# Zero gaps between the score tiles of a fused attention and long-convolution kernel, with a rebuilt start and a new instruction order

## The chip, the cores and the metric

The kernel runs on one core of one Trainium2 chip. The metric is the time of one execution in microseconds (us), as a median of several runs. A second number, the span, is the time from the first to the last instruction in one profiled execution.

The core has a matrix engine (PE; its weight loads are shown apart as PEld), a vector engine (DVE), a scalar engine with lookup tables (ACT), a general engine (POOL) and an engine that only issues transfers (SP). POOL, SP and ACT can start DMA transfers.

## The reference

Four batches of 768 positions, 8 heads of 64. First a local attention with 8 global keys, then a gated long convolution.

```python
scores = scale * q @ k.T - slopes[h] * dist      # dist: position difference, or 96 for a global key
keep   = (key < 8) | ((0 <= rel) & (rel < 96))   # rel = query - key
x      = softmax(where(keep, scores, -1e9)) @ v  # heads side by side: [4, 768, 512]
x1, x2, x3 = split(x @ w_proj)                   # 512 columns each
y      = x1 * irfft(rfft(x2) * rfft(filter)) * x3
out    = y @ w_out
```

## The kernel before, in words

**Attention.** The keys of a batch are cut into seven tiles of 112 (K0); the upper 112 rows of a 128-row tile hold them, the lower 16 rows hold the 8 global keys and zeros. Queries that such a tile can see are at most 208, so its scores form a strip of 208 columns (96 for the last tile), and a head's strips stand side by side in the tensor E, 208 apart. Tiles come in three groups (GRP): 0 and 1; 2 and 3; 4, 5 and 6. For each group and pair of heads there is a step "scores" (PE), one "exp" (ACT, L711) and, from batch 1 on, a "masked" product with exp(-slope x distance) (DVE, L718). In batch 0 the masks don't exist yet, so the biases are added inside PE: L688 multiplies a scaled identity ("slope", L516 to L523) by copies of the distance table dg ("near", L505 to L514).

"values" (L728 to L743) multiplies strips by v, with the E strip as weights: for query tile t first 128 columns of strip t (L736), then, for t > 0, the last 96 columns of strip t-1 (L741), which land on rows 0 to 95 of the same bank.

**q and k** must be transposed to QT and KT. In batches 0 to 2 PE does it (L628 for the first tiles, which come as fp32; L661 for the rest). In batch 3 SP does it with transposing DMAs ("crossed", L650). QT and KT exist once, so a transposed tile may be written only when the batch before has read the old one. Parts of x are transposed by SP as well (L792).

**Convolution.** After attention come the gates (L827), the projection (L901), a transform as matrix products (L615), the products with the filter's spectrum on DVE, the inverse (L926, L929), and the output projection (L953); ACT and DVE empty the PSUM banks between them (L305, L309, L311, L836).

**Order.** Every step is an operation with a number, given by its place in the code. ORDER lists all of them by hand; "84P45" is operation 84 on engine P with PSUM banks 4 and 5, and the letters are P, A (ACT), V (DVE), G (POOL) and S (SP); "i22b0" is 22 idle matmuls. So ORDER fixes, for each engine, which steps it does and in which sequence, and an engine never passes a waiting step. Counting the operations through the code gives each number its name.

**Start.** DVE clears idle, the slope tensor, the lower rows of k and v (L392, L394, L1092) and the spare columns of E (L399); POOL builds an identity and dg (L479 to L486) and then issues loads; SP loads q tiles 2 and 1, k tile 0, the first rows of v and q tile 0; PE runs 22 idle matmuls. The first ACT step is a sine, which brings the sine table; the exp table follows at the first exp, the sine table again for the transform's tables (L420), and the exp table again for the masks (L539).

Of the kernel before, what the change touches and what calls it, by code (L numbers as in the profile page):

```python
# [11 lines left out]
BF16 = mybir.dt.bfloat16  # L12
# [4 lines left out]
P = 128  # L17
# [23 lines left out]
0V 1V 5G 2A 23G 32V 37A 41G 6A 7V 45G 46G 8V 40A 36A 9V 24V 33A 35A 47G 44G 11V 39A 25G 52G 50G 19S 51G 53G 13V 18S  # L41
26A 43G 29A 42G 49G 48G 58G 27A 17S i22b0 78P0 34A 74P1 10V 76P2 75V 77V 28V 56G 79A 55G 54G 3G 31V 57G 20S 254G 4V
80P0 30A 81A 16S 72P3 73A 82A 12V 38A 255G 104P1 105A i1b2 106P2 84P45 107V 108P3 109V 90P01 14V 83V 102P3 103V 59G
88P67 86P23 85A 89A 110P45 87A 15V 152P6 153V 148P7 149V 112P23 91A 111A 150P6 113A 114P01 115A 154P7 116P45 253G 21V
151V 155V 162P67 117A 63V 158P01 22V 97P45 98V 163A 99V 156P23 123P67 124V 159A 157A 68A 92P01 93V 125V 251G 94V 66A
118P45 119V 100P2 61G 101V 208P3 126P6 209A 120V 127A 213P7 160P01 95P2 214A 210V 121P6 96V 164P45 252G 122V 134P6
161A 169P01 128P2 211V 165V 166V 167P3 64A 212A 129P4 353P5 170V 215V 216V 217A 171V 136A 168V 172P0 133P3 71A 135A
220P1 221A 62G 70A 138P6 130A 354V 173V 179P3 175P0 131V 60G 201V 355A 180P5 69A 194V 202V 195V 197V 65A 203V 132V
262G 174P2 140A 204V 196V 198V 182A 222V 177A 263G 143P4 278P6 205V 219V 261G 223A 224A 349P0 145A 260G 266G 206V 137V
351P5 199V 287P7 207V 200V 276P4 225A 268G 181A 350V 352V 176A 279A 357P23 289P6 356A 218V 183V 277V 288A 274P7 363P45  # L50
226V 360P01 358A 67A 290A 484G 267G 364A 227V 359V 366P23 367A 291P6 292A 282P4 283A 228V 275A 256G 139P5 229V 381P6
382A 190P4 144P7 379P6 185P2 192A 230V 231V 232V 178V 425P4 233V 380V 234P3 269G 146A 257S 389P67 426V 141A 392P45
361A 259G 483G 187A 482G 386P01 362V 365V 265G 241P2 142V 242V 235A 184P3 393A 368V 264G 387A 388V 280P4 390A 281A
147V 236P2 427P5 186A 428V 429P0 430V 391V 189P1 374P45 375V 237A 481G 191A 383P67 440P23 480G 384A 293P0 258S 441A
489G 394V 376V 385V 581P1 294A 369P67 370V 239P4 582V 442V 240A 295P5 296A 371V 431P23 432A 395P01 396V 377P4 378A
490G 583V 492G 579P5 397V 577P6 580V 302P7 243V 303A 437P23 438A 434P01 578V 400P45 238V 372P7 401V 373A 402V 491G
607P6 435A 248P23 398P7 608V 403P4 404A 193V 609P5 272G 399V 300P6 249A 250A 271G 301A 270G 495G 439V 244P01 436V 245A
488G 406P4 420P2 421P3 707G 297V 708G 246A 610A 408A 433V 298V 423A 651P0 285V 448P67 449V 496G 652V 450V 410P1 588P45
411P3 188V 247V 304V 422A 412A 584A 589A 413A 443P01 444V 611P67 612A 445V 299V 585P45 415P2 586A 451P3 452A 416P6
591P45 592A 594P01 595A 305V 498G 446P7 447V 405P3 407A 473V 474V 417A 500G 320P4 321A 469P7 485G 705G 418A 312P5  # L60
620P01 313A 617P23 459P4 284V 471A 461A 419V 308P5 464P6 621A 618A 466A 497G 653P4 487S 316P7 317A 286V 310P0 475V
710G 476V 477V 306P1 716G 717G 309A 314P2 318P6 307A 319A 587V 706G 478V 519P7 493G 593V 463P1 479V 315A 409V 654A
655P6 656A 720G 590V 311V 465A 454P5 517P4 714G 805S 424V 614P01 520A 486S 804S 803S 666P23 725G 456A 660P67 502P5
414V 518A 661A 712S 830S 596V 322V 615A 468P4 323V 613V 667A 521P6 504P7 470A 505A 324V 657P01 616V 325V 709G 503A
806S 273G 668V 663P23 664A 523P4 515P7 831S 658A 828S 715G 453P5 455A 619V 326V 721G 506P2 507A 622V 718G 329V 330V
597P01 598V 522A 524A 327V 458P5 599V 460A 516A 494G 626P23 510P6 508P4 509A 802S 511A 627V 665V 328V 807V 829S 340P5
341A 628A 832A 600P4 601V 623P01 602P67 346P5 347A 603V 337P4 808P23 624V 338A 625V 604V 814P01 815A 662V 501G 811P67
659V 526V 874S 809A 530P5 525V 343P4 499G 669P01 722G 531A 812A 629S 816V 344A 672P23 331P5 332A 605P4 606A 457V 673V
670V 674V 528P6 529A 334P7 467V 833P45 817P23 671V 875S 335A 839P01 834A 818A 462V 810V 532V 630S 472V 873S 642P6 644A
646P7 648A 713G 527V 636P4 638A 813V 631P5 836P67 842P23 840A 512V 843A 533V 637P4 719G 639A 513V 647P0 649A 819V 711S  # L70
633A 723G 632P1 726G 641P4 837A 514V 844V 823P23 546P5 841V 643A 820P67 542P4 835V 824V 825V 675S 634A 848P01 547A
543A 548P5 333S 549A 544P4 876S 877A 540P2 821V 822V 849V 676S 850V 545A 650V 677S 698V 699V 701V 640V 645V 826S 827S
541A 534P3 535A 342S 887P67 881P45 884P01 888A 889V 694P2 689P3 536P6 882A 883V 700V 885A 679P7 681A 693P4 696A 838V
537A 695A 683P5 702V 724G 635V 538P7 539A 703V 684P2 688P4 690A 685A 886V 845P67 878P01 879A 731P4 846V 732A 550V 551A
678P5 847V 851S 880V 893P01 691A 680A 727P4 728A 704V 890P67 552V 742P5 894V 744P4 852S 895A 891V 892V 896S 745A 553V
743V 729P3 730A 753P6 754A 336S 740P5 741A 554V 339S 748P4 555V 556V 749A 746P3 747A 733P6 755P5 735P7 864P4 697V
859P3 751V 869P0 736A 854P7 863P1 756A 565P5 734A 871A 562P0 750V 752V 692V 868P6 757V 865A 897S 737V 758V 769P1 686V
687V 566A 557V 770A 898S 773P5 738V 739V 559P2 861A 774A 682V 856A 771P3 563A 765P5 766A 761P1 763P7 870A 919V 759P0
760A 914P5 853P6 920V 922V 767P0 921V 866A 872V 855A 762A 764V 930P4 916A 768A 772A 923V 943P1 924V 925V 939P0 940A
926P3 560A 561S 927A 941P0 954P2 944A 928P3 858P1 775V 776V 952P5 558V 955A 915P2 777V 778V 779V 780V 942A 947P0 929A  # L80
931A 953A 956V 948A 781V 957V 945P3 568P5 946A 949V 950V 932P0 933A 348S 574P3 575A 951V 934P0 935A 345S 569A 571P4
782V 917A 905P3 973P5 790P2 784P0 860A 937V 567S 791A 974A 936V 960P2 785A 867V 564S 918V 786S 938V 977P1 961A 862V
964P5 965A 783V 978A 975P0 971P2 958P7 972A 962P5 963A 857V 787P1 976V 979V 904P5 980V 959A 966V 967A 981V 982V 968V
983V 986V 900P0 899P2 576S 969V 788A 572A 573S 907A 910P1 912A 987V 970V 984V 985V 906A 902V 909P4 911A 908V 913V
793P3 901A 799P1 796P2 991P4 903V 800A 570S 999V 794A 994P3 997V 1000V 789S 797A 792S 998V 798S 801S 795S 995V 988P2
992A 993S 989A 996S 990S 1007P4 1008V 1009S 1004P5 1005A 1006S 1001P2 1002A 1003S
"""


class Bank:  # L90


    def __init__(self):
        self.left, self.at = 0, None
        self.tile, self.users, self.owner = None, [], None
# [1116 lines left out]
```

## Time and profile before

| what | value |
|---|---|
| median of 3 runs | 172.23 us (172.14 to 172.71) |
| profiled execution, its own time | 174.0 us |
| its span | 171.4 us |
| busy: PE, DVE, ACT, POOL | 162.9, 153.1, 148.5, 72.8 us |
| granted PE clock | full throughout |
| shares of the chain that ended last | PE 84%, ACT 7%, DMA 4% |
| values matmuls | L736 x224, L741 x192 |

Matmuls are pipelined and the ends that the profile gives them are modelled, so two neighbours overlap in it; the distance between two starts tells what one costs. "L711 ACT ACTIVATE E<-bank" is line 711 on ACT, which writes E and reads a bank. A line such as L305 can be that of a helper that many steps share. Releasers ("what ended the wait") are inferred. SPq is SP's transfer queue: its entries are the issuing, not the transfer.

### The profile page before, as it was taken

Reading aid. Unit: us, or ns where it says so; the run is one execution under the profiler, and the core shown is the slowest. Engines: PE = TensorE matmul, PEld = TensorE weight load, DVE = VectorE, ACT = ScalarE, POOL = GpSimd, SP = SyncE. Lnnn points to the kernel's source line nnn. Section 1 sums busy time; section 2 is a strip of 40 time slices with the busy share of each in tenths; the row PEclk is TensorE's granted clock in tenths of the full one; section 3 lists DMA queues with packets and bytes.
Section 4 is the critical chain, followed back from the end, with each engine's and each line's share of the span. In section 5 each row is a group of like instructions: output and inputs, shape, how many; then the busy total and the mean of one; then the engine's idle time right before and its main releaser. Section 6 shows DMA issues by size and latency. Waiting matters only on the chain.

```text
span 171.4 us, 4261 instructions
## 1 busy us (share of the span) xinstructions
PE 162.9 (95%) x1623; PEld 102.8 (60%) x1623; DVE 153.1 (89%) x326; ACT 148.5 (87%) x293; POOL 72.8 (42%) x99
## 2 busy tenths in 40 slices
PE   7999999999999999999997699999999999999990
PEld 2567878654656876675564465866645755466440
DVE  7579878999999999999996879999799999999960
ACT  7699999999999999999998689898996779788741
POOL 7999999529996699958700000000000000000000
PEclk9999999999999999999999999999999999999999
DMA  5999999999999999999999635112251004303686
GB/s 126 183 145 144 146 161 190 195 176 156 156 165 154 87 131 150 144 157 165 134 145 156 122 67 145 23 31 88 57 170 29 2 0 177 134 0 124 245 316 235
DMA packets 96452, 22.85 MB, mean 133 GB/s; under 512 B 89352, under 2 KB 93360, under 8 KB 96432
## 3 DMA queue, kind: packets, MB, share of 16 engines
q0 software_dynamic: 75952, 11.95, 99.8%
q1 hardware_dynamic: 20480, 10.63, 25.5%
q8 instruction: 12, 0.20, 0.5%
q14 instruction: 8, 0.07, 0.1%
HBM read 24.92 MB, written 6.29 MB: 182 GB/s over the span
## 4 chain that ended last, share of the span: by engine, by line
PE 84%; ACT 7%; DMA 4%; issue 1%; DVE 1%; DVEq 0%
PE bank L827 21%; PE bank L901 12%; PE bank L953 11%; PE bank L697 6%; PE bank L615 6%; PE bank L926 5%; PE bank L741 5%; PE bank L736 4%; DMA QT<-qn 4%; PE bank L301 4%; PE bank L661 4%; PE bank L688 2%; PE bank L782 2%; ACT mask L539 2%; ACT E L711 1%
## 5 line engine op out<-in xcount | busy, mean ns | idle before, releaser
L827 PE MATMUL bank<-xT,w 128*128 128x384 f16 x256 | 47.8, 326 | 0.0
L711 ACT ACTIVATE E<-bank 128x832 f16<-128x832 f32 (+1 forms) x48 | 42.0, 954 | 2.6 <-PE bank L697 2.4
L827 PEld LDWEIGHTS <-w 128*128 128x128 f16 x256 | 23.7, 98 | 16.0 <-issue 0.9
L321 POOL DMA_DIRECT2D kn<-in_k_dram x27 | 22.5, 837 | 5.7 <-PE bank L661 5.3
L953 PE MATMUL bank<-wo,y 128*128 128x512 f16 x96 | 23.0, 379 | 0.7 <-DVE xT L305 0.7
L321 POOL DMA_DIRECT2D vn<-in_v_dram x28 | 23.3, 841 | 0.6 <-DMA wo<-in_moe_w_out_dram 0.6
L718 DVE TENSOR_TENSOR E<-E,mask 128x832 f16<-128x832 f16 (+1 forms) x36 | 21.5, 616 | 0.2 <-ACT E L711 0.2
L321 POOL DMA_DIRECT2D qn<-in_q_dram x21 | 18.8, 902 | 4.7 <-PE bank L661 3.2
L741 PE MATMUL bank<-vn,E 128*96 128x65 f16 x192 | 18.1, 206 | 0.0
L736 PE MATMUL bank<-vn,E 128*128 128x65 f16 x224 | 18.1, 196 | 0.0
L309 ACT ACTIVATE ot<-bank 128x512 f32<-128x512 f32 x22 | 12.9, 602 | 5.9 <-PE bank L953 5.9
L309 ACT ACTIVATE x<-bank 128x384 f16<-128x384 f32 x32 | 16.1, 531 | 2.0 <-PE bank L827 0.9
L736 PEld LDWEIGHTS <-E 128*128 128x128 f16 x224 | 16.6, 108 | 1.7 <-DVE KT L305 0.2
L760 DVE TENSOR_TENSOR xn<-bank,rc 128x512 f16<-128x512 f32 (+1 forms) x22 | 16.8, 770 | 0.3
L741 PEld LDWEIGHTS <-E 128*96 128x96 f16 x192 | 16.5, 126 | 0.6
L697 PE MATMUL bank<-QT,KT 64*128 64x208 f16 (+1 forms) x224 | 14.7, 244 | 2.0 <-DMA QT<-qn 1.6
L953 PEld LDWEIGHTS <-y 128*128 128x128 f16 x96 | 9.2, 98 | 10.6 <-issue 1.0
L305 ACT CAST eo<-bank 128x384 f16<-128x384 f32 x29 | 13.4, 509 | 1.8 <-PE bank L929 1.7
L305 ACT CAST X<-bank 128x512 f16<-128x512 f32 x24 | 13.7, 596 | 1.4 <-PE bank L615 1.3
L836 ACT CAST g<-bank 128x384 f16<-128x384 f32 x29 | 14.2, 518 | 0.5 <-PE bank L827 0.4
L309 ACT ACTIVATE ab<-bank 128x512 f16<-128x512 f32 x22 | 13.4, 641 | 1.0 <-PE bank L901 0.9
L697 PEld LDWEIGHTS <-KT 64*128 64x128 f16 x224 | 8.8, 94 | 7.8 <-issue 2.9
(149 smaller groups left out, 332.8 us busy)
## 6 DMA issues: line engine op xcount, KB each, us to landing
out_dram<-ot SPq DMA_DIRECT2D x24, 256.0 KB, 2.7
vn<-in_v_dram POOLq DMA_DIRECT2D x28, 112.0 KB, 5.5
kn<-in_k_dram POOLq DMA_DIRECT2D x27, 112.0 KB, 5.6
qn<-in_q_dram POOLq DMA_DIRECT2D x21, 128.0 KB, 5.8
w<-in_moe_w_proj_dram POOLq DMA_DIRECT2D x4, 256.0 KB, 5.9
ot<-in_q_dram SPq DMA_DIRECT2D x3, 256.0 KB
g<-in_moe_filter_fft_dram POOLq DMA_DIRECT2D x1, 768.0 KB, 11.1
w<-in_moe_w_proj_dram POOLq DMA_DIRECT2D x1, 512.0 KB, 8.2
```

Of the source, the lines that this page charges most:

```text
L305: {"A": nc.scalar.copy, "V": nc.vector.tensor_copy, "G": nc.gpsimd.tensor_copy}[e](out, in_)
L309: self.nc.scalar.mul(out, in_, c)
L321: return self.g.op(eng, 0.57 + 0.00035 * nbytes[0] if eng == "G" else 0.5, lambda _: e.dma_start(dst, src), w=w, r=r, nbytes=nbytes, name= ...
L697: nc.tensor.matmul(bs[hh].f32()[:, off:off + w], self.KT[hs, hp, P * m:P * m + P], self.QT[hs, hp, KL * m:KL * m + w], start=(off == 0 and ...
L711: g.op("A", act(2 * W), lambda _: nc.scalar.activation(eo, bs[0].two()[:, :, 0:W], Act.Exp, scale=self.scale), use=bs, w=[("E", hp, gi)], ...
L718: g.op("V", dve(2 * W, 2), lambda _: nc.vector.tensor_mul(eo, eo, mk), r=[("mask", 2 * hp), ("mask", 2 * hp + 1)], w=[("E", hp, gi)], name ...
L736: nc.tensor.matmul(o[:, n, hh], ef[:, at:at + P], vt[:, t, 2 * hp + hh, 0:D + 1], start=first, stop=(t == 0), skip_group_check=True)
L741: nc.tensor.matmul(o[0:self.LAST, n, hh], ef[:, at:at + self.LAST], vt[:, t - 1, 2 * hp + hh, 0:D + 1], start=False, stop=True, skip_group ...
L760: nc.vector.tensor_mul(to, o[:, :, :, 0:D].rearrange("p i (t h) d -> p i t h d", h=2), rc.rearrange("p i (t h) o -> p i t h o", h=2).to_br ...
L827: nc.tensor.matmul(bk.f32()[:, 0:h], self.w[:, c, o + P * j:o + P * j + P], self.xT[:, c, h * s:h * s + h], start=(c == 0), stop=(c == 3))
L901: nc.tensor.matmul(bk.f32(), src[:, c], w[:, c, DM:2 * DM], start=(c == 0), stop=(c == 3))
L953: nc.tensor.matmul(bk.f32(), y[:, c, P * t:P * t + P], self.wo[:, c, :], start=(c == 0), stop=(c == 3))
```

## The change

- E: strips are 224 apart instead of 208 (the last two, tiles 5 and 6, stay 208 apart), with 16 zero columns between them. The second values matmul takes 128 columns instead of 96 and writes all 128 rows. The exp of group 2 becomes two instructions; masks are 752 wide instead of 720.
- slope: filled from the identity for the first pair of heads only; the other three pairs are that one times a constant.
- near: dg itself serves as one half of the bias operand; near is two copies of dg with its halves swapped, and a small tensor edge holds the special first strip. Broadcast views replace repeated columns.
- zero rows: memsets of k's and v's lower rows become three DMAs on SP that read idle; the memset of ones comes after them.
- The first ACT function is exp. q tiles 1 and 2 are loaded by ACT's queue, k tile 0 and q tile 0 by SP's. 17 idle matmuls instead of 22.
- ORDER is new throughout. On POOL the loads of q3, q4, k2, k1, k3 come before dg; group 1 of batch 0 is computed before group 0; the transposing DMAs of batch 3 stand as k0 k1 (two copies) q0 k2 q1 q3 q2 k4 k3 q4 instead of k0 (copy) q2 q1 (copy) k2 k1 k3 q3 q0 q4; some evacuations change between ACT and DVE.

```diff
-    XB = (3,)
+    XB = ((3, 0), (3, 1), (3, 2))
-    N, LAST = 208, 96
+    N, LAST, STEP = 208, 96, 224
+    E0 = [224 * t for t in range(6)] + [1328]
...
-        g.op("A", 0.2, lambda _: nc.scalar.activation(self.warm, self.warm, Act.Sin),
+        g.op("A", 0.2, lambda _: nc.scalar.activation(self.warm, self.warm, Act.Exp),
...
-        for lo, hi in ((0, 2), (2, 7)):
-            g.op("V", dve(512 * (hi - lo), 2), lambda _, lo=lo, hi=hi: v.memset(self.kn[0:LO, lo:hi], 0.0),
...
+        g.op("V", dve(256), lambda _: v.memset(self.EE[:, :, :, 1424:1456], 1.0), w=ew, name="gaps")
+        g.op("V", dve(640), lambda _: v.memset(
+            self.EE[:, :, :, 0:1120].rearrange("p a b (t c) -> p (a b) t c", t=5)[:, :, :, self.N:], 0.0), w=ew, name="gaps")
...
+            g.op("AV", {"A": act(e) + 0.05, "V": dve(e, 4) + 0.05}, lambda en, ps=ps, other=other: self.copy(
+                en, near[ps], dg[other]), r=["dg"], w=[("near", half)], bias=-2900, name="near")
...
+            g.op("AV", {"A": 0.32, "V": 0.25}, lambda en, ps=ps, half=half, dst=dst: self.times(
+                en, dst, self.ident[ps, None, ps].to_broadcast([64, 2, 64]), self.slopes[half] / self.scale),
+                r=["ident", "slope"], w=[("slope", 0, half)], name="slope")
+        for hp in range(1, 4):
+            g.op("AV", {"A": act(256) + 0.05, "V": dve(256, 4) + 0.05}, lambda en, hp=hp: self.times(
+                en, self.slope[:, hp], self.slope[:, 0], self.slopes[2 * hp] / self.slopes[0]),
+                r=[("slope", 0, half) for half in range(2)], w=[("slope", hp)], name="slope")
...
+        if gi < 2:
+            eo = et[:, :, at:at + 2 * self.STEP].rearrange("p h (t c) -> p h t c", t=2)[:, :, :, 0:n]
+            parts = [(eo, lambda: bs[0].two()[:, :, 0:W].rearrange("p h (t c) -> p h t c", t=2), 2 * W)]
+        else:
+            parts = [(et[:, :, at:at + n], lambda: bs[0].two()[:, :, 0:n], 2 * n),
+                     (et[:, :, self.E0[5]:self.E0[5] + W - n], lambda: bs[0].two()[:, :, n:W], 2 * (W - n))]
...
-                            at = self.N * (t - 1) + KL
-                            nc.tensor.matmul(o[0:self.LAST, n, hh], ef[:, at:at + self.LAST],
+                            at = self.E0[t - 1] + KL
+                            nc.tensor.matmul(o[:, n, hh], ef[:, at:at + P],
...
-            self.g.op("V", dve(3584, 2), lambda _, vt=vt: v.memset(vt[0:LO, :, :, 0:D], 0.0),
+            self.load("S", vt[0:LO].rearrange("p t h d -> p (t h d)").rearrange("p (a b) -> p a b", a=12),
+                      self.idle[0:LO, None, 0:448].to_broadcast([LO, 12, 448]),
...
+        for eng, what, o, src, t, p0 in (("S", "q", 0, self.q, 0, 0), ("A", "q", 1, self.q, 1, 0),
+                                         ("S", "k", 3, self.k, 0, LO), ("A", "q", 2, self.q, 2, 0)):
+            self.load_first32(eng, what, o, src, t, p0)
+        self.load("S", self.kn[0:LO].rearrange("p t h d -> p t (h d)"), self.idle[0:LO, None].to_broadcast([LO, 7, 512]),
...
```

## The prediction, made before the result was known

> **What bounds the kernel now.** I read the table of busy time by stage first, since a share over the whole span mixes a start, a long full part and a tail.
>
> ```profile
> 0.00:12.00 12.00, 10.74 (x65) 6.03 (x67) 8.33 (x25) 9.38 (x25) 10.98 (x24) 1.00 1.46 152
> 12.00:40.00 28.00, 27.75 (x392) 19.79 (x390) 25.16 (x61) 27.46 (x45) 22.67 (x30) 1.00 1.86 167
> 40.00:60.00 20.00, 19.61 (x236) 12.90 (x235) 19.60 (x42) 19.40 (x33) 17.09 (x21) 1.00 2.17 143
> 60.00:80.00 20.00, 20.00 (x220) 13.70 (x219) 19.64 (x41) 19.62 (x41) 17.95 (x22) 1.00 2.05 149
> 80.00:100.00 20.00, 17.67 (x203) 10.68 (x198) 16.78 (x37) 17.21 (x35) 4.06 (x5) 1.00 1.87 136
> 140.00:160.00 20.00, 20.00 (x122) 11.13 (x121) 19.38 (x40) 16.45 (x37) 0.00 (x0) 1.00 0.30 110
> ```
>
> Columns: stage, its length, then busy us (instructions) of PE, PEld, DVE, ACT, POOL, granted clock, DMA share, GB/s. From 12 to 40 us ACT is full (27.46 of 28). From 40 to 80 PE, DVE and ACT are all full: 39.6, 39.2 and 39.0 of 40. From 80 to 100 all three have holes, PE 2.33 us. After 100 PE is full, DVE nearly, ACT has 15 to 20% free.
>
> Next the chain that ended last, at its two places that are not PE or ACT work:
>
> ```profile
> 11.26 0.59 ACT QT L305
> ...
> 11.86 1.28 ACT L711
> 13.16 0.48 ACT E L711
> ...
> 88.22 6.79 DMA QT<-qn
> 95.01 0.71 issue
> 95.72 0.71 PE bank L697 x12
> ```
>
> Columns: start, us, what. The first exp waits for a table load (L711, 1.28 us) although its scores were ready by about 11.5. At 88.22 to 95.72 the scores of batch 3 wait for a transposed q tile. SP's own timeline says why it comes late:
>
> ```profile
> 80.04 2.63 SPq L650 DMA_TRANSPOSE QT<-qn  x2
> 82.79 0.71 SPq L321 DMA_DIRECT2D vn<-vn  x1
> 83.60 4.46 SPq L650 DMA_TRANSPOSE KT<-kn  x3
> 88.22 5.01 SPq L650 DMA_TRANSPOSE QT<-qn  x3
> ```
>
> By ORDER these are q2 q1, a copy, k2 k1 k3, then q3 q0 q4. The first could start only when batch 2's last scores of group 1 had read QT; q0 stands seventh and lands at 95.0, about 15 us later. PE had only 13.1 us of work in ORDER between those scores and batch 3's first.
>
> Last, the values matmuls, whose second one has 96 weight columns:
>
> ```profile
> L736 PEld LDWEIGHTS <-E 128*128 128x128 f16 x224 | 16.6, 108 | 1.7 <-DVE KT L305 0.2
> L741 PEld LDWEIGHTS <-E 128*96 128x96 f16 x192 | 16.5, 126 | 0.6
> ```
>
> The narrower load takes longer (126 against 108 ns). The starts in PE's timeline agree: where L736 and L741 alternate, twelve L741 start from 63.37 to 64.21, 76.4 ns a pair; in group 0, with two L736 to one L741, they start at 86.72, 86.83, 86.94 and 87.04, 107 ns a triple. So an L736 more costs 30 ns and an L741 some 46.
>
> **The change part by part.** Against the profiled execution: span 171.4, its own time 174.0 (2.6 around the span), the median of the runs 172.23. I sum differences in the span and put them on the median.
>
> *Full-width weights.* 192 loads grow to 128 columns, each step falling from 46 to 30 ns: 16 ns each. The 48 of batch 0 lie in the ACT-bound start and give nothing; 144 x 16 = **-2.2** (bounds 0 and -2.2). Price: two gap memsets instead of one (256 elements take 0.27 us, so 640 more 0.3 to 0.7, on DVE before 8 us, hidden), masks 752 instead of 720 wide (8 x 0.03 us), and the exp of group 2 becomes two. ACT's evacuations take 0.596 us for 512 and 0.509 for 384 elements, which leaves 0.25 fixed; two of 384 start 0.37 apart (37.41 to 38.15), so 0.14 of it overlaps the neighbour and 0.11 stays: 16 x 0.11 = 1.8 us on ACT, counted below. Strided E writes and products: no row has them alone; between 0 and 5% of the 21.5 us of L718; I take 0, since element count and types stay.
>
> *The start.* ACT loses the eight slope fills of 0.30 us and the eight copies into near (1.5 + 1.8 us), and gets four small ones (1.2) and about an evacuation more: some 4 us less before the first exp. DVE loses four zero memsets, 0.49 + 1.13 + 2 x 1.55 = 4.7 us, and gets the near copies (nearest rows: the copies of dg at L533 and L535, 0.31 and 0.92; I take 0.6 each), the edges and a slope or two. The exp table goes to the idle time before the first transposes: its 1.28 us leave the path. So ACT is ready; what is late next is DMA and DVE. ORDER puts the loads of q3 q4 k2 k1 k3 on POOL ahead of dg, which takes 2.07 us there: they are issued 2 us earlier, k2 at about 3.1. It was issued at 5.17 before and its transpose waited for it until 10.3, so it now lands at 8.2. The SP queue gets two zero DMAs ahead of q0 (0.4 to 0.5 us of issue each by its rows); q0 still lands before 9.5, and only the last transpose before the scores needs it. ACT's queue issues q2 and q1 before any ACT work: hidden. The five idle matmuls less are hidden, as PE then waits for k2. Behind k2 DVE must evacuate KT2 (8.9), finish dg (0.75), near twice (1.2), QT4 (0.4) and QT2 (0.69): 11.9; scores 0.5; first exp at 12.4 instead of 13.16, **-0.8** (bounds -1.6 with 0.3 us copies, +0.6 with slow copies and a late k2). The wait added here, ones on the zero rows, has the next evacuations behind it on DVE, but the zeros land by 8 us and DVE gets there at 12.
>
> The Trainium skill, page "ScalarE: Activation LUTs", section "What ACT_TABLE_LOAD costs", says that a switch costs 2.66 us with its drain. The trace disagrees: the load is 1.28 and the exp starts 0.01 later. By the page the start would gain 1.38 more.
>
> From first exp to batch 1's first exp ACT took 26.3 us (13.16 to 39.42). Counted through both ORDERs it now holds four split exps (+0.48), wider masks (+0.2), an xT copy (+0.55) and the twin copy (+0.55) more, and an ab (0.54), a KTg (0.3), two inverse tables (0.7) and two x evacuations (0.86) less: **-0.6**. Start in all **-1.4** (bounds -3 and +1).
>
> *The crossing.* The new SP order is k0 k1, two copies, q0, then k2 q1 q3 q2. The first five wait only for loads and for group 0 of batch 2; behind batch 2's last group-1 scores stand four transposes of 1.5 us, and 5.1 us to land (q0: issued 89.9, landed 95.0): 11.1 us. PE has 13.1 us of work there, as before. q2's load is the 74th of 87 on POOL; the 74th was issued at 70.3 and would land at 76. So the wait goes: **-2.3**, PE's hole (bounds 0 and -3).
>
> *Give-back.* In 40 to 85 us DVE and ACT are as full as PE. Half of the values gain falls there (72 x 16 ns) and gives nothing by itself: **+1.1**. ORDER also moves work: DVE gets two X, one ab, two x, two KT and a mix step, and loses two eo, an ot, a spectrum copy, QT, KTg and twin: net +1.3 by the rows (0.64 for 512 from PSUM, 0.5 for 384, 0.6 for KT); ACT loses about as much and gets 1.3 of split exps. **+1.3** (give-back's bounds 0 and 4.6).
>
> Sum: -1.4 - 2.2 - 2.3 + 1.1 + 1.3 = -3.5; 172.23 - 3.5 = **168.7**. The tail after 160 us (outputs, evacuation, store) has the same form: 0.
>
> **The rivals.**
> *The wait stays* (171.0): batch 3's loads or the copies ahead of q0 come later than I place them, and another transpose is last. For it: SP is in order and two copies wait for v loads. Against: 2 us to spare.
> *The start and the values come through whole* (166.3): no give-back. For it: after 100 us ACT is 15% free, and DVE has 4.7 us less at the start. Against: DVE full from 40 to 80.
> *DVE becomes the bound* (174.3): of the moved work its receipts, X 1.3, ab 0.6, x 1.5 and KT 1.2 = 4.6 us, fall into 40 to 96 and what it loses lies after 100, so PE waits for banks that DVE must empty, and the hole at 88 is only DVE's time to catch up. Then -1.4 - 1.1 + 4.6 = +2.1. It decides as soon as more than 2.5 us net come to DVE there. For it: 39.2 of 40 us busy. Against: my count gives half of that.
> *Wider loads cost more* (172.0): if a load's time went with its columns, 126 ns would become 168 and the step 61 instead of 46: +2.2 instead of -2.2, no 1.1 given back: -1.4 + 2.2 - 2.3 + 1.3 = -0.2. Against it stand the 108 and 126 ns above, in the same sequence. The page "TensorE: Matmul & The Clock Gate" of the Trainium skill, section "LDWEIGHTS (loading the stationary operand)", states that rule, P/1.2 ns for P columns; the trace goes against it.
> *A second table load* ahead of the first exp, if the slope fills choose another table: 1.28 us back, 170.0, inside the forecast's own range.
>
> **How the numbers follow.** Forecast 168.7 (own range 167.0 to 170.5) 0.45; wait stays 0.15; all comes through 0.12; DVE bound 0.18; wider loads 0.03; parts cancel within 0.3% 0.07. About 0.3% (0.5 us) is what a measurement of this kernel can tell from no change. Faster 0.72, same 0.10, slower 0.18. The range leaves out the DVE rival only and takes in the large gain and the start's bad bound: 166.0 to 172.6.
>
> **What would show it.** L741's loads near 108 ns and pairs 61 ns apart; one table load before 12 us and the first exp at 12.4; batch 1's first exp near 38; no DMA piece of microseconds in the chain between 80 and 100. I am wrong if first exps start after 13, if rc, xn or bank waits on DVE fill the chain in 40 to 100, or if PE's hole moves to another QT or KT tile.

## The result, and the profile after

| | before | changed |
|---|---|---|
| median | 172.47 us (172.14 to 172.94, 4 runs) | 180.66 us (178.29 to 183.55, 4 runs) |
| ratio, 95% interval | | 1.043 [1.032, 1.053]: slower |
| profiled execution: its time, span | 174.0, 171.4 us | 180.85, 179.1 us |
| mean granted PE clock | 1.00 | 0.97 |
| first exp of batch 0, 1, 2, 3 | 13.16, 39.42, 65.71, 96.29 us | 19.40, 44.43, 70.99, 98.97 us |
| PE idle from 80 to 110 us | 2.33 us | 5.50 us |

168.7 was forecast. Ratios here and below leave out disturbed executions and medians do not, so that the two can differ by up to 1%. Line numbers have grown: L661 is now L663, L697 L704, L711 L726, L736 L755, L741 L760, L827 L846, L953 L972, L650 L652, L792 L811; the helpers L305, L309, L321 are L307, L311, L323.

The table of milestones already splits the loss. 6.2 us are lost before the first exp, 3.6 of them are won back until batch 3's first exp, and another 5.0 are lost after it (80.1 us to the end instead of 75.1).

Busy time by stage of the changed kernel (columns as in the prediction):

```profile
0.00:12.00 12.00, 5.58 (x17) 2.02 (x17) 2.36 (x13) 2.60 (x6) 10.07 (x21) 0.98 1.43 158
12.00:40.00 28.00, 26.81 (x372) 20.91 (x373) 22.02 (x57) 23.86 (x40) 21.34 (x28) 0.89 1.73 152
60.00:80.00 20.00, 19.91 (x270) 14.72 (x268) 19.82 (x43) 19.65 (x41) 18.19 (x22) 1.00 1.87 124
80.00:100.00 20.00, 18.68 (x180) 10.14 (x179) 19.37 (x41) 18.57 (x44) 9.16 (x12) 1.00 1.97 135
100.00:110.00 10.00, 5.82 (x75) 3.34 (x74) 7.55 (x15) 4.53 (x10) 0.00 (x0) 0.86 1.43 178
```

By 12 us PE has been busy 5.2 us less than before, the clock of 12 to 40 is 0.89 instead of 1.00, 60 to 80 is as full as it was, and a new hole opens at 100. POOL, which was nearly done with loading at 80 (4.06 us left), now has 9.16 us left. The chain that ended last names both holes:

```profile
3.34 9.80 DMA kn<-in_k_dram
...
13.19 1.03 PE bank L663 x8
```

```profile
76.61 13.13 DMA vn<-in_v_dram
...
90.03 9.55 DMA kn<-in_k_dram
...
99.61 5.96 DMA KT<-kn
...
106.33 0.43 ACT xT L307
...
106.81 1.56 PE bank L972 x4
```

And the profile's groups name what PE waited for:

```profile
L972 PE MATMUL bank<-wo,y 128*128 128x512 f16 x96 | 23.1, 385 | 4.2 <-ACT xT L307 4.2
L704 PE MATMUL bank<-QT,KT 64*128 64x208 f16 (+1 forms) x224 | 15.2, 251 | 1.4 <-DMA QT<-qn 1.3
```

The first hole is K tile 2 of batch 0, 9.8 us on its way. The second hole is K tile 3 of batch 3, whose crossing (its transposing DMA) on SP starts at 99.61 and lands at 105.6; ACT's copy of the global keys waits for it, two evacuations wait behind the copy, and PE waits 4.2 us for the second of them. Ahead of that PE still waits 1.3 us for a Q tile, which is what the kernel before lost there (1.6 us). One row of it misleads: the chain pairs the landing at 99.6 with a load issued at 90.03. Counted through ORDER, that is K tile 5's load. Tile 4's was issued at 81.68 and tile 3's at 84.93, and they took 16.6 and 14.7 us until their crossings could start. SP's timeline has the gap that this leaves:

```profile
85.38 6.95 SPq L652 DMA_TRANSPOSE QT<-qn  x3
98.32 2.86 SPq L652 DMA_TRANSPOSE KT<-kn  x2
101.28 1.20 SPq L811 DMA_TRANSPOSE xT<-xn  x1
```

What POOL waited for between 60 and 100 us says more:

```profile
POOL kn L323 <- DMA vn<-in_v_dram: 4.3, 1, 4.3
POOL vn L323 <- DMA vn<-in_v_dram: 3.4, 2, 1.8
POOL kn L323 <- DMA wo<-in_moe_w_out_dram: 2.3, 1, 2.3
```

These 10 us are waits for earlier transfers: POOL sits with its loads undone because those ahead haven't landed. It waited for a buffer that PE was still reading for only 2.9 us. In the kernel before, waits for transfers were 0.6 us in this stretch, and waits for PE 2.0.

The values steps did what was forecast:

```profile
L755 PEld LDWEIGHTS <-E 128*128 128x128 f16 x224 | 14.1, 97 | 2.2 <-DVE E L737 0.5
L760 PEld LDWEIGHTS <-E 128*128 128x128 f16 x192 | 13.2, 97 | 0.7
```

97 ns instead of 126 and 108; where the two alternate, fourteen pairs start from 59.96 to 60.81, 61 ns a pair (76.4 before, 61 forecast).

### The profile page after: what moved, and what is told of

It reads as the page before. It is cut to its first block, busy times and chain, and to the rows that moved or that the text cites. A ratio compares the mean times of both kernels' runs of the same rounds, so it can differ in the third digit from the quotient of the medians.

```text
span 179.1 us, 4204 instructions
## 1 busy us (share of the span) xinstructions
PE 162.1 (91%) x1593; PEld 100.4 (56%) x1593; DVE 148.5 (83%) x327; ACT 143.8 (80%) x297; POOL 73.0 (41%) x99
## 3 DMA queue, kind: packets, MB, share of 16 engines
q1 hardware_dynamic: 18944, 10.57, 26.6%
## 4 chain that ended last, share of the span: by engine, by line
PE 50%; DMA 21%; ACT 14%; POOL 9%; issue 3%; DVE 1%; POOLq 0%; ACTq 0%; DVEq 0%
PE bank L846 13%; DMA kn<-in_k_dram 11%; PE bank L972 10%; DMA vn<-in_v_dram 7%; PE bank L920 6%; PE bank L945 4%; POOL vn L323 3%; PE bank L617 3%; DMA KT<-kn 3%; PE bank L704 3%; ACT E L726 3%; POOL qn L323 3%; ACT mask L541 3%; PE bank L663 3%; PE bank L693 2%
## 5 line engine op out<-in xcount | busy, mean ns | idle before, releaser
L846 PE MATMUL bank<-xT,w 128*128 128x384 f16 x256 | 48.6, 329 | 0.0
L726 ACT ACTIVATE E<-bank 128x832 f16<-128x832 f32 (+2 forms) x64 | 44.0, 799 | 2.2 <-PE bank L704 2.1
L846 PEld LDWEIGHTS <-w 128*128 128x128 f16 x256 | 23.6, 98 | 15.9 <-issue 1.5
L323 POOL DMA_DIRECT2D kn<-in_k_dram x27 | 22.4, 839 | 13.6 <-PE bank L663 5.5
L972 PE MATMUL bank<-wo,y 128*128 128x512 f16 x96 | 23.1, 385 | 4.2 <-ACT xT L307 4.2
L323 POOL DMA_DIRECT2D vn<-in_v_dram x28 | 23.8, 864 | 3.7 <-DMA vn<-in_v_dram 3.4
L323 POOL DMA_DIRECT2D qn<-in_q_dram x21 | 19.2, 926 | 4.4 <-PE bank L846 3.4
L311 ACT ACTIVATE ot<-bank 128x512 f32<-128x512 f32 x23 | 13.8, 612 | 4.6 <-PE bank L972 4.5
L972 PEld LDWEIGHTS <-y 128*128 128x128 f16 x96 | 9.1, 98 | 14.5 <-issue 5.1
L704 PE MATMUL bank<-QT,KT 64*128 64x208 f16 (+1 forms) x224 | 15.2, 251 | 1.4 <-DMA QT<-qn 1.3
L855 ACT CAST g<-bank 128x384 f16<-128x384 f32 x30 | 15.3, 525 | 1.0 <-PE bank L846 0.9
L311 ACT ACTIVATE x<-bank 128x384 f16<-128x384 f32 x29 | 14.7, 517 | 0.9 <-ACT E L726 0.6
L755 PE MATMUL bank<-vn,E 128*128 128x65 f16 x224 | 15.3, 193 | 0.1
L755 PEld LDWEIGHTS <-E 128*128 128x128 f16 x224 | 14.1, 97 | 2.2 <-DVE E L737 0.5
L307 ACT CAST eo<-bank 128x384 f16<-128x384 f32 x31 | 14.1, 534 | 1.3 <-PE bank L948 0.9
L760 PE MATMUL bank<-vn,E 128*128 128x65 f16 x192 | 15.1, 193 | 0.0
L307 DVE COPY KT<-bank 128x448 f16<-128x448 f16 (+1 forms) x11 | 5.3, 490 | 10.9 <-PE bank L663 10.9
L311 ACT ACTIVATE ab<-bank 128x512 f16<-128x512 f32 x21 | 12.9, 661 | 1.5 <-PE bank L920 1.5
L704 PEld LDWEIGHTS <-KT 64*128 64x128 f16 x224 | 9.0, 96 | 9.0 <-issue 6.9
L760 PEld LDWEIGHTS <-E 128*128 128x128 f16 x192 | 13.2, 97 | 0.7
```

The lines of the kernel that those rows point to most:

```text
L307: {"A": nc.scalar.copy, "V": nc.vector.tensor_copy, "G": nc.gpsimd.tensor_copy}[e](out, in_)
L311: self.nc.scalar.mul(out, in_, c)
L323: return self.g.op(eng, 0.57 + 0.00035 * nbytes[0] if eng == "G" else 0.5, lambda _: e.dma_start(dst, src), w=w, r=r, nbytes=nbytes, name= ...
L704: nc.tensor.matmul(bs[hh].f32()[:, off:off + w], self.KT[hs, hp, P * m:P * m + P], self.QT[hs, hp, KL * m:KL * m + w], start=(off == 0 and ...
L726: nc.scalar.activation(dst, src(), Act.Exp, scale=self.scale)
L755: nc.tensor.matmul(o[:, n, hh], ef[:, at:at + P], vt[:, t, 2 * hp + hh, 0:D + 1], start=first, stop=(t == 0), skip_group_check=True)
```

## The experiments

Words like 713G are ORDER's; "..." stands for what is not moved.

Times inside an execution come from one profiled execution for each kernel, and the same start does not come out the same each time. K tile 2's first transpose came at 13.19 us in the changed kernel, and at 12.01, 12.60 and 13.56 in three runs below that leave the start alone, with first exps at 17.39, 17.96 and 18.91. With the start of the kernel before it came between 10.1 and 11.3 in five. So a difference of 1 us at the start, seen once, says nothing.

### The start: clock, order or transfers

**Idle matmuls in the gap.**

```diff
-i17b0
+i46b0
```

> The changed kernel with 46 instead of 17 idle matmuls at the start, so that TensorE's 6.4 us without work are filled with work that nobody needs. Theory 'clock' (the granted clock of 0.50 and 0.70 after the gap stretches the first transposes and scores): the granted clock stays at 1.00 until 20 us, the stretch from K tile 2's landing to the first scores falls from 5.5 to about 3.5 us, the first exp comes near 17.4 and the time is 178.5 to 179. Rival (the evacuations on ACT and VectorE or later loads set that stretch): the first exp stays within 0.7 us of 19.4 and the time within 0.7 us of 180.7.

178.81 us, ratio 1.035 [1.023, 1.046]. The granted clock was 1.00 to 160 us, the first exp came at 16.67, batch 1's at 41.70. PE's first transpose of K tile 2 was at 12.94, and from there to the first exp it took 3.73 us instead of 6.21: some 2.5 us of the late first exp are the clock after the gap. The rest is K tile 2's late landing. Of 2.7 us won at the first exp 0.6 were left at batch 3's (98.38), and 1.9 in the median, which is not clear of the noise (the intervals overlap).

**The fp32 tiles first.**

```diff
-i17b0 102P0 ... 98P1 ... 7V ... 74P2 ... 70P3 ... 100P0 ... 72P4
+i17b0 7V 74P2 70P3 72P4 102P0 ... 98P1 ... 100P0
```

> The changed kernel with the fp32 tiles (K tile 0, Q tiles 1 and 2) transposed ahead of K tile 2 and Q tiles 3 and 4 on TensorE, and the memset that K tile 0 needs moved up with them; no transfer is moved. Theory 'everything is late' (the fp32 tiles on SyncE's and ACT's queues are held up by the same crowd): TensorE's first tile comes at 9 to 12 us, the first exp within 1 us of 19.4 and the time within 1 us of 180.7. Theory 'only POOL's queue is late': the fp32 tiles are there at 7 to 9 us, 2.6 us of fp32 transposes go into the gap, the clock stays higher, the first exp comes near 17 and the time is 178 to 179.

179.46 us, 1.039 [1.032, 1.045]. The fp32 tiles were there at once: PE worked on them from 6.74 to 8.21 us. Then it waited until 13.01 for K tile 2, and the clock was 0.50 from 12 to 18 all the same. First exp 18.23. Only POOL's queue is late; PE's order is not the cause.

**The zero rows by memset.**

```diff
-            self.load("S", vt[0:LO]..., self.idle[0:LO, None, 0:448]..., "zeros", r=["idle"])
+            self.g.op("V", 2.0, lambda _, vt=vt: v.memset(vt[0:LO, :, :, 0:D], 0.0), ..., name="zeros")
-        self.load("S", self.kn[0:LO]..., self.idle[0:LO, None]..., "zeros", r=["idle"])
+        self.g.op("V", 2.0, lambda _: v.memset(self.kn[0:LO], 0.0), ..., name="zeros")
-... 19S ... 11S ... 13S
+... 19V ... 11V ... 13V
```

> The changed kernel with its three zero-row transfers made VectorE memsets again, each at its old place in the order. Theory 'zeros' (the zero rows crowd the first loads out of the DMA engines): batch 0's K tile 2 lands near 10.3 us as in the kernel before instead of 13.1, the first exp comes near 16.5 instead of 19.4, and the time falls from 180.7 to 177 to 178. Theory 'share' (a third queue, ACT's, takes a third of the packets from POOL's loads): K tile 2 still lands between 12.5 and 13.2 and the time stays within 1 us of 180.7. In both the DVE memsets add 2 to 3 us of DVE work before 20 us.

178.97 us, 1.033 [1.023, 1.042]. PE's first transpose of K tile 2:

```profile
9.79 0.58 PE L663 MATMUL bank<-ident,kn 128*128 128x128 f16 x4 [2.31 <-DMA kn<-in_k_dram]
```

3.4 us earlier than in the changed kernel; first exp 15.13. It was 9.79 to 9.92 in all five runs with every zero row by memset, and never below 12 with the transfers and ACT's queue. "Share" falls as the cause of this delay: ACT still has a queue of its own here. The memsets of vn then held DVE in front of the bias and KT steps that PE needed (ACT waited 2.7 us for scores at 21 us), and batch 1's first exp was at 44.26, hardly earlier.

**Only kn's zero rows by memset.**

```diff
-... 19S
+... 19V
```

> The changed kernel with the zero rows of kn alone by a VectorE memset (as before the change); the zero rows of both vn buffers stay transfers. With all three as memsets K tile 2 was there at 9.7 to 9.9 us, but the two vn memsets (1.55 us each at 13.7 and 19.9) then held scores for 3 us. Theory 'kn's zeros': they alone crowd K tile 2; it lands at 9.5 to 10.3, the first exp comes near 14, no DVE memset stands between 13 and 22 us, batch 1's first exp comes near 39.5 to 40.5 (44.4 in the changed kernel) and the time is 176.5 to 178 with the second stall still there. Rival 'all zero rows': K tile 2 lands at 11.5 to 13 and batch 1's first exp stays above 42.5.

179.69 us, 1.031 [1.024, 1.038].

```profile
12.73 0.58 PE L663 MATMUL bank<-ident,kn 128*128 128x128 f16 x4 [6.34 <-DMA kn<-in_k_dram]
```

The rival holds: 12.73 lies among the times of the unchanged start, so vn's zeros are enough by themselves, and taking kn's away changes nothing that can be seen. No run takes away vn's alone. Batch 1's first exp was at 43.80. The packets of the first 16 us, queue by queue, show the exchange. Changed kernel (queue: packets, MB, time share):

```profile
q0 software_dynamic: 8089, 1.02, 117.1%
q1 hardware_dynamic: 2568, 0.97, 35.6%
```

All zero rows by memset:

```profile
q0 software_dynamic: 10319, 1.30, 127.5%
q1 hardware_dynamic: 2024, 0.51, 17.2%
```

q0 is POOL's queue, q1 SP's. 544 packets of zeros, some 850 bytes each, stand where 2230 of POOL's packets, of 126 bytes, could. The Trainium skill, page "DMA: Bandwidth & Descriptors", section "Queues, rings and completion order", says that a DMA engine serves its queues in turn, a packet at a time; the trace agrees so far that big packets of one queue cost another many small ones. Whether the packets that the profile counts are those that the page means, it does not show.

**Two queues at the start.**

```diff
-... 18A ... 16A
+... 18S ... 16S
```

> The changed kernel with the loads of Q tiles 1 and 2 issued by SyncE instead of ACT, at the same places in the order, so that two queues load at the start as in the kernel before. Theory 'share': POOL's queue has half the packets again, K tile 2 lands near 10.3 us, the first exp comes near 16.5 and the time falls to 177 to 178. Theory 'zeros' or a total that is bound whatever the queue: K tile 2 lands at 12.5 to 13.5 us and the time stays within 1 us of 180.7.

179.22 us, 1.027 [1.015, 1.039]. PE began K tile 2 at 10.57, now waiting last for kn's zeros, and the next two K tiles came only at 14.54. With Q tiles 1 and 2 ahead of them on SP the zeros start later and hit the next loads instead. That K tile 2 comes earlier is no proof of "share", which the run with memsets had refuted. First exp 16.28. A smaller share may still be there: with all memsets K tile 2 took 6.5 us from its issue (3.34 to 9.79) and 5.1 us in the kernel before (5.17 to 10.3), where two queues loaded. No run has memsets and two queues together.

**All zero rows by memset, vn's moved up to where DVE waits.**

```diff
-... 34V 103V ... 11V ... 13V
+... 34V 11V 13V 103V
```

> The changed kernel with all three zero-row transfers as VectorE memsets, and the two of vn moved up VectorE's order to where it waits 5.3 us for the first transposes, so that they hold nothing. Theory 'the zero rows of vn crowd the first loads': K tile 2 lands at 9.7 to 9.9 us, no clock drop, the first exp comes near 13.6 and batch 1's first exp at 39 to 39.5 (44.4 in the changed kernel, 42.0 with the memsets at their old places); the time is 176 to 178 because the stall at 100 to 105 us swallows most of it. Rival 'the start is the whole loss': 175 or less with no other edit.

176.92 us, 1.012 [1.002, 1.021]. K tile 2 at 9.84; batch 1's first exp 40.23, later than expected because the clock dropped in the profiled execution (0.89 from 12 to 20 us). The run's interval lies below that of the changed kernel: the start is a large part of the loss, not the whole.

### Parts of the change in the kernel before

**Full-width values alone.** Gaps, wide masks, split exp and 128-column weights in the kernel before:

```diff
-                            at = self.N * (t - 1) + KL
-                            nc.tensor.matmul(o[0:self.LAST, n, hh], ef[:, at:at + self.LAST],
+                            at = self.E0[t - 1] + KL
+                            nc.tensor.matmul(o[:, n, hh], ef[:, at:at + P],
```

> The kernel before, in its own order, with the zero gaps in E, full-width stationary operands in the values, the split exp of the last group and the wider masks, and nothing else of the change. The prediction's terms for this part were -2.2 for the values and +1.1 given back by ACT and VectorE: about 171.4 us beside 172.5. If nothing is given back 170.3; if ACT's second exp and the longer masks decide, 172.5 to 173. A changed kernel whose loss comes from the start and from its new order alone keeps this row at or below 172.5.

170.58 us, 0.984 [0.975, 0.993]: faster, by 0.7 to 2.5%. First exps 12.91, 38.95, 64.70, 93.30; the group that was L741:

```profile
L757 PEld LDWEIGHTS <-E 128*128 128x128 f16 x192 | 13.2, 97 | 0.6 <-issue 0.2
```

A gain of some 2 us is the -2.2 of the prediction without its give-back of 1.1.

**The exp table first, on top of it.**

```diff
-        g.op("A", 0.2, lambda _: nc.scalar.activation(self.warm, self.warm, Act.Sin),
+        g.op("A", 0.2, lambda _: nc.scalar.activation(self.warm, self.warm, Act.Exp),
```

> The kernel before with the full-width values of the run before-wide, and the exp table in place of the sine table as ACT's first table load; nothing else. ACT's chain QT, table load 1.28 us, first exp loses the table load: the first exp moves from 12.9 to about 11.7 us; the sine table still has to be loaded once and exp once again after the sines, as now. If the start's gain is kept to the end: 170.6 - 1.2 = 169.4 us. Rival: ACT is not the bound in 12 to 40 us, or a later transfer swallows it: within 0.5 us of 170.6.

171.08 us, 0.990 [0.984, 0.996]: no gain over the run before it that these runs can tell. The first exp came 0.85 us earlier, although K tile 2 came 0.5 us later (10.64, 10.11): from its transpose it was 1.42 us instead of 2.80, so the 1.28 us of the load did leave the path. But ACT's next exp then waited for PE, and batch 1's first exp was at 39.21 (38.95 without the edit). L723 is the exp in this kernel, L701 the scores:

```profile
12.06 0.87 ACT L723 ACTIVATE E<-bank 128x832 f16<-128x832 f32 x1
13.93 2.38 ACT L723 ACTIVATE E<-bank 128x832 f16<-128x832 f32 x3 [1.00 <-PE bank L701]
```

**Batch 3's K tile 3 late, in the kernel before.** (717G, 831S and 832A are its load, its crossing and the key copy there.)

```diff
-... 717G ... 831S ... 832A ... 722G 629S ... 833P45
+... 717G 722G 831S 629S ... 832A 833P45
```

> The kernel before with one thing of the new order put in: batch 3's K tile 3 is the 81st of POOL's 87 loads instead of the 68th (80th in the changed kernel), and its crossing on SyncE stands ahead of x tile 2's as there. Theory 'late issue': SyncE waits for the load with the x crossings behind it, TensorE gets a hole of 2 us or more at 95 to 108 us, and the time rises by 1.5 to 4 us, to 174.3 to 177. Rival 'it only follows from the late start': the load is there in time, and the time stays within 0.7 us of 172.8.

174.66 us median (171.96 to 175.49), too wide for a verdict. The trace speaks for the rival: the load, now issued at 80.75 us, was there when SP came to it, and PE's idle time from 80 to 110 was 1.77 us (2.33 before). A late place by itself opened no hole here; whether it costs some time, these runs can't tell.

### The second hole

The expectations put the issue of K tile 3's load at 90 us, by the chain's row above; 84.93 is right.

**Batch 3's K tiles 4 and 3 loaded earlier.**

```diff
-269G ... 717G ... 713G
+717G 713G 269G
```

> The changed kernel with the loads of batch 3's K tiles 4 and 3 issued on POOL ahead of the load of w_out, 10 to 12 issues earlier; nothing else moved. Theory 'late issue' (the second stall, 100 to 107 us, is there because K tile 3's load is the 80th of 87 and is issued at 90): it is issued near 77 and lands near 90, its crossing no longer ends last, TensorE is busy for 9 us or more of 100 to 110, and the time falls by 3 to 5 us to 176 to 177.5. Rival 'the transfers as a whole are late' (the same bytes in another order): the stall moves to a QT tile or to batch 3's V tiles and the time stays within 1.5 us of 180.

177.95 us, 1.026 [1.019, 1.033]. Some 3 us better in the median. The profiled execution is 4.4 us shorter, of which 2.0 lie at the start, which the edit does not touch, and only 1.4 behind batch 3's first exp (78.7 us to the end, 80.1 in the changed kernel). The hole went elsewhere, as the rival said: PE was idle 2.97 us from 80 to 110, most of it for the crossing of Q tile 4,

```profile
PE bank L704 <- DMA QT<-qn: 2.1, 1, 2.1
```

then for x tile 3, and the clock was 0.50 for 3.4 us behind it.

**ACT's key copy later.**

```diff
-... 828A 340A
+... 340A ... 602A ... 597A ... 828A 832P45
```

> The changed kernel with ACT's copy of the global keys of batch 3's group 1 (which waits 4.5 us for the crossed K tile 3) moved down ACT's order, behind the evacuations of two out tiles and of two xT tiles, directly ahead of the group's scores. Theory 'the copy blocks ACT': TensorE no longer waits for xT at 102.6 to 106.8 and about 3 us of other work fills the gap; the time falls by 2 to 3 us. Rival: the scores of group 1 come so soon behind that the wait is only handed to them, and the time falls by less than 1 us.

177.70 us, 1.029 [1.023, 1.035]. PE no longer waits for ACT's xT, and 0.4 us for the crossed one; the scores wait 2.0 us for the copy instead, and the clock drops behind that. The median is nearer to the theory, but of the 3.2 us by which the profiled execution is shorter 1.4 lie at the start (first exp 17.96), which the edit does not touch; the hole itself stays.

**Zero rows by memset (at their old places) and the K tiles earlier.**

> The changed kernel with the zero rows by VectorE memsets again and batch 3's K tiles 4 and 3 loaded earlier, both edits as in their own runs. The memsets alone brought the first exp from 19.4 to 15.1 us, but the time only from 180.7 to 179.0. Theory 'the late K tiles swallow what the start gains': together they give 180.7 - 4.3 - 3 = 173 to 174. Rival 'the transfers as a whole are late': together 177 or more, with the stall at another tile.

177.39 us, 1.016 [1.008, 1.024]: no 173. First exp 13.64, but the vn memsets at 13.68 and 19.90 (1.55 us each) cost PE 3.0 us and batch 1 began at 42.03; and at 100 to 110 PE still lost 2.0 us to Q tile 4's and x tile 3's crossings.

**x tile 3's crossing ahead of Q tile 4's,** on top of the early K tiles and kn's zero rows by memset.

```diff
-625S ... 825S ... 832P45 829P01 ... 331A ... 626S 642P3 638P2
+625S ... 626S 825S ... 331A 642P3 638P2 832P45 829P01
```

> The changed kernel with kn's zero rows by memset, batch 3's K tiles 4 and 3 loaded 10 to 12 issues earlier, and at the end of batch 2 the crossing of x tile 3 ahead of Q tile 4's on SyncE, with an out tile's evacuation and two of batch 2's gates ahead of batch 3's group 1 scores on TensorE. Theory 'two stalls and the clock behind each': TensorE is busy for 9 us or more of 100 to 110 at a clock of 0.95 or more, and the time is 171 to 174. Rival 'transfers as a whole are late': the hole of 2.5 us at 101 to 104 in the run with the early K tiles stays, at another tile, and the time is 175 or more.

179.55 us, 1.038 [1.031, 1.044]: worse than with the early K tiles alone. x tile 3's crossing took 7.0 us and now ends last; kn's zeros by memset again didn't help the start (first exp 18.66). A miss on both counts: this order of the crossings doesn't help while each of them is slow.

**Two queues besides** (18A and 16A as 18S and 16S).

> As the run just before it, with the loads of Q tiles 1 and 2 on SyncE's queue besides. Theory 'share' and 'zeros' both act: K tile 2 lands at 8.2 to 9 us, as the prediction had it, the first exp comes at 12.4 to 13.2, and the time is 0.5 to 1.5 us below the run just before it, 170.5 to 173. Rival 'only the zero rows crowd': K tile 2 lands where it does in the run just before it, within 0.4 us, and so does the time within 0.7 us.

177.23 us, 1.015 [1.006, 1.023]. K tile 2 at 10.33, K tiles 1 and 3 at 14.36, as in the run with two queues alone: neither answer in full, since the zeros only move on to the next loads.

**Memsets moved up, K tiles earlier.**

> The same with batch 3's K tiles 4 and 3 loaded 10 to 12 issues earlier. Theory 'two causes, both settled': batch 1's first exp at 39 to 39.5 us, batch 3's near 93, the hole at 100 to 105 is below 1.5 us, the clock stays at 1.00 and the time is 170 to 172.5. Rival 'the last loads are late whatever K tile 3 does' (POOL still issues V tiles until 95 us, and the crossings of Q tile 4 and x tile 3 take 4 to 6 us beside them): the hole stays at 2 to 3 us with its clock drop and the time is 173.5 to 176.

174.29 us (12 runs), 1.008 [1.004, 1.011]. First exps 13.58, 38.60, 65.15 and 93.40, all as expected. But PE's idle time from 80 to 110 was 5.3 us, for QT, xT and crossed x, although no K tile was late: the rival's time. POOL's waits in 60 to 100 were again for transfers, the longest single one, 3.3 us, for w_out. That led to the last theory.

**w_out loaded earlier, on top of it.** 269G is w_out, 512 KB; a K, Q or V tile is 112 or 128. It moves to a place where POOL waits for PE anyway.

```diff
-705G ... 717G 713G 269G
+269G 705G ... 717G 713G
```

> As the run with early memsets and early K tiles, with the load of w_out moved 17 issues up POOL's order, to where POOL waits 2.75 us for TensorE (at 53 to 56 us). There POOL's last loads each waited for a transfer issued eight loads earlier, the longest (3.3 us) for w_out, and the last was issued at 90 us instead of 84. Theory 'the last loads end late': the wait for w_out goes, the last load is issued by 87 us, TensorE's idle time of 80 to 110 us falls from 5.3 to about 3 us and the time from 174.3 to 172.5 to 173.5. Rival 'the transfers together are the bound, or the order of the work around 100 us': the last load is issued at 89 to 91 us all the same, or the hole stays at 4.5 us or more; the time is 173.7 to 175.

170.35 us, 0.986 [0.982, 0.990]: 1.0 to 1.8% faster than the kernel before, and 2 us more of a gain than the theory had. POOL's last load is issued at 86.57, and of POOL's waits for transfers from 60 to 100 us one kind is left:

```profile
POOL vn L323 <- DMA qn<-in_q_dram: 2.6, 2, 2.2
```

The stages:

```profile
80.00:100.00 20.00, 18.52 (x210) 10.73 (x204) 19.93 (x41) 17.94 (x42) 4.61 (x6) 1.00 1.74 141
100.00:110.00 10.00, 10.00 (x108) 6.73 (x108) 8.90 (x19) 9.70 (x20) 0.00 (x0) 1.00 0.48 105
```

PE's hole from 80 to 110 is 1.48 us, and no wait for a QT or KT tile is left in PE's list. From batch 3's first exp to the end it is 75.7 us (75.1 before, 80.1 in the changed kernel).

**w_out alone moved, in the changed kernel.**

```diff
-705G ... 269G
+269G 705G
```

> The changed kernel with the load of w_out moved as in the run just before this one, and nothing else: zero rows by transfer, K tiles 4 and 3 at their late places. Theory 'POOL's last loads wait for w_out's transfer': K tile 3's load is issued by 86 us instead of 90, TensorE is busy for 8 us or more of 100 to 110, the late start of 6 us stays, and the time falls from 180.7 to 176 to 177.5. Rival 'the K tiles' places decide as well': K tile 3 is still the 80th load, the hole behind it stays at 3 us or more and the time is 178 to 180.

175.68 us, 1.012 [1.007, 1.017]: one edit takes back 3 of the 4.3 per cent, with the late start (first exp 18.91) and K tiles 4 and 3 in their late places, behind the same number of tiles. They are now issued without a wait:

```profile
82.55 3.49 POOL L323 DMA_DIRECT2D kn<-in_k_dram  x4
```

and their crossings go out from 91.9 to 95.0 instead of 98.3 to 101.2, with no wait of SP for kn:

```profile
91.92 3.12 SPq L652 DMA_TRANSPOSE KT<-kn  x2
```

From batch 3's first exp to the end it is 75.4 us. PE's idle time from 80 to 110 is 0.99 us, without a wait for a Q or K tile; another 1.7 us are lost at 60 to 80, to V tiles that now stand behind w_out.

**w_out earlier in the kernel before, with full-width values.**

```diff
-707G ... 273G
+273G 707G
```

> The kernel before with the full-width values and the load of w_out moved up to where POOL waits for TensorE at 53 to 57 us. There POOL waited only 0.6 us (before) or not at all (with the full-width values) for w_out, and TensorE lost 0.7 to 2.3 us at 80 to 110 us. Theory 'w_out's transfer also slows the crossings there': 0.5 to 1 us, to 169.6 to 170.1. Rival 'it is only POOL's wait that counts': within 0.4 us of 170.6.

170.77 us, 0.983 [0.976, 0.989], the same as without: there w_out stood behind batch 3's K tiles 0 to 3, and its transfer held back nothing that was due soon.

**What follows.** Two causes, each shown by itself. (1) The zero rows as transfers, vn's being enough, hold up POOL's first loads by 2 to 4 us (3.4 in the changed kernel), and the gap halves PE's clock until 18.4. (2) In the new order w_out's 512 KB go into POOL's queue just ahead of batch 3's last tiles, K tiles 4 and 3 land 15 to 17 us after their issue, and the crossings run beside the rest of the loads. That w_out's place decides is shown: with nothing else moved K tile 4, issued at 82.55, was there by 91.92. How the queue spends the time is not: POOL's wait for w_out was over at 84.93, and K tile 4 needed until 98.3. With both mended, and K tiles 4 and 3 loaded early besides, the changed kernel is 1.4% faster than the one before, and no better than the full-width values alone (0.986 and 0.984): the remaining edits are worth nothing that these runs can tell.

## Why the prediction was wrong, point by point

- *Full-width weights, -2.2*: right in mechanism and size (97 ns, 61 ns a pair, 2 us by itself). "Wider loads cost more" was wrong, and so is here the rule P/1.2 of the Trainium skill (page "TensorE: Matmul & The Clock Gate", section "LDWEIGHTS (loading the stationary operand)"): a load of 96 columns took 126 ns, one of 128 takes 97 (by the rule, as an estimate, 80 and 107).
- *The start, -1.4*: the step that failed is "its transpose waited for it until 10.3, so it now lands at 8.2". I moved the landing with the issue and priced the zero transfers by their issue alone (0.4 to 0.5 us on SP). They cost K tile 2 another 3.4 us (13.19 against 9.79); and even without them it lands at 9.8, not 8.2, for a reason that stays open. From its landing to the first exp I had 4.2 us; undisturbed it was 3.7 (9.85 to 13.58). What I left out altogether is the clock: PE waited 6.4 us, and some 2.5 of the 6.2 us at the first exp are that.
- *The exp table first*, most of the -0.8: right for the first exp (0.85 us), but nothing is left of it one exp later.
- *ACT's stretch, -0.6*: it was -1.2 (25.03 instead of 26.26 us from first exp to batch 1's).
- *The crossing, -2.3*: "So the wait goes" failed. PE's wait for a Q tile only fell from 1.6 to 1.3 us, and a wait of 4.2 us came behind it. The 5.1 us to land were misread (I split a row of three evenly; q0 was issued at 90.66, which leaves 4.3), but q2's crossing, issued at 90.79, was not there before 98.67, nearly 8 us later. I followed q2's load, the 74th of POOL's 87 steps, and not those of K tiles 4 and 3, the 79th and 80th, which SP also has ahead of x tile 2; and I took a load's landing to be 5 to 6 us wherever it stands. Behind w_out it was 15 to 17. "PE's hole moves to another QT or KT tile", my sign of error, is what the trace shows. With w_out out of the way the wait for QT does go.
- *Give-back, +2.4 in all, and "DVE becomes the bound"*: not seen. From batch 1's first exp to batch 3's the changed kernel took 54.5 us, the one before 56.9, and that one with the full-width values alone 54.4: the work that ORDER moves costs nothing that shows there.
- *Second table load*: there is only one load ahead of the first exp, at 1.36 us, far off the path.

The range took in none of this, because its worst start was +1: no rival asked what transfers do to each other.

## What to carry to other kernels

Here a transfer that was moved or added was paid by those in flight beside it and behind it in its queue. So before counting a landing time at a new place, list what else is queued there in bytes, and look first for the largest item (here w_out, whose place alone was worth 3%). Wait rows on the issuing engine that name a DMA meant here that eight loads were out; look then for a big load that could go where that engine waits anyway. And a hole of PE had a second price here, the clock behind it. Compare also the parts of a kernel that an edit leaves alone: here the first exp of the same start moved by up to 2 us between executions.

## What the runs showed of the hardware

**The clock.** In a hole or behind it the granted clock fell to 0.50 for a stretch of 3.4 us, or twice that: 11.58 to 18.40 and 107.14 to 110.56 in the changed kernel, 104.56 to 107.96 with the early K tiles, worked out from rows of 1 us. Two executions with the same start show that a short hole may or may not do it. A hole of 2.33 us (K tile 2 at 9.92; w_out earlier):

```profile
9.00:10.00 1.00, 0.08 (x2) 0.11 (x3) 0.00 (x0) 0.00 (x0) 1.00 (x2) 0.91 2.42 154
10.00:11.00 1.00, 1.00 (x10) 1.00 (x10) 0.46 (x2) 0.03 (x1) 1.00 (x2) 0.50 2.42 154
13.00:14.00 1.00, 1.00 (x14) 0.99 (x13) 0.86 (x2) 0.58 (x3) 1.00 (x2) 0.89 1.63 103
```

and one of 2.83 us (K tile 2 at 9.85; the run without that edit):

```profile
10.00:11.00 1.00, 1.00 (x15) 1.00 (x14) 0.70 (x2) 0.51 (x2) 1.00 (x2) 1.00 2.43 155
```

The column ahead of the last two is the clock: 0.91, 0.50, 0.89 against 1.00. It cost 1.7 us at the first exp (15.26 and 13.58). Counted from the start of the last idle matmul, whose end is modelled, the two holes are 2.71 and 3.21 us. The Trainium skill, page "TensorE: Matmul & The Clock Gate", section "Part 1: The HAM clock gate (the "warmup" mystery)", speaks of a free-running window of some 3.4 us, with which length and chance agree. Its section "HAM oscillation — how this bites in real kernels" warns of gaps above 3.4 us; here 2.33 were enough.

**POOL's loads in flight.** Where POOL waited for a transfer between 76 and 100 us, it was the eighth load ahead, counted through ORDER in the changed kernel (K tile 3 for w_out, K tile 5 for a V tile of batch 2): with eight out, the next isn't issued. Whether the chip or the program's own bookkeeping sets the eight, no run shows.

**Transposing transfers beside loads.** SP's crossings of Q and K tiles landed 4.1 us after their issue at best (the kernel before) and 9.8 at worst (early memsets and early K tiles), as the profile pairs them. For x tiles two runs show the contrast: 7.02 us for a crossing issued at 97.62, beside 3767 packets of POOL's queue (x tile 3 moved up), and 2.90 us for one issued at 102.67, beside 11 (late key copy).
